# Backward attention of a two-block network: dq and dk accumulated in one pass, and the gradient of q, k, v passed on through DRAM

## The chip, the cores and the metric

The kernel runs on one core of a Trainium2 chip. The metric is device time in microseconds (us) for one launch: the median of several executions. The profile is taken from one further execution, which has a time of its own.

In what follows PE is the matrix engine, DVE the vector engine, ACT the scalar engine, POOL and SP the two others, which here mostly issue transfers. PSUM is the memory that PE writes its results to, in float32; SBUF is the large on-chip memory. DRAM is the chip's main memory.

## The reference

Four residual blocks, A, B, A, B, on x of shape [1, 2048, 576] in bf16, and the gradient of the result with respect to x and all five weights. Block A is attention with 32 heads of 18 elements, in which each position looks at itself and seven earlier ones at a distance of two:

```python
W, dil = 8, 2
q, k, v = qkv[0], qkv[1], qkv[2]
off = jnp.arange(W) * dil
idx = pos[:, None] - off[None, :]
mask = idx >= 0
kg = k[:, :, idx_c, :].reshape(B, H, S, W, Dh)
vg = v[:, :, idx_c, :].reshape(B, H, S, W, Dh)
logits = jnp.einsum("bhsd,bhswd->bhsw", q, kg) * scale
attn = _softmax(jnp.where(mask, logits, -1e9), axis=-1)
o = jnp.einsum("bhsw,bhswd->bhsd", attn, vg)
```

Block B is a bilinear unit with 4608 hidden columns: (x Wg) * (x Wu), times Wd. Both blocks are preceded by a layer norm without weights.

For the backward pass of A let dl[s,w] be the gradient of the logits. Then dq[s] = scale * sum over w of dl[s,w] * k[s-2w], dk[s] = sum over w of dl[s+2w,w] * q[s+2w], with the scale folded into the stored q, and dv[s] = sum over w of attn[s+2w,w] * do[s+2w]. The sum for dq reads k shifted back; those for dk and dv gather from later positions. The gradients of q, k and v together, called dqkv, are multiplied by the transposed weights to give dh, the gradient of the layer norm's output, and are used once more at the end for the weight gradients.

## The kernel before

The kernel runs forward through the layers, and then backward: layer 3 (B), layer 2 (A), layer 1 (B), layer 0 (A). The weight gradients of B and then of A come last. The change lies in the backward pass of A, `layer_A_bwd` (L640), which runs twice, for l=2 and l=0.

Feature rows are laid out transposed: features on partitions, positions along a row. The 576 features form five chunks, four of 126 rows (seven heads) and one of 72 (four heads). The 2048 positions form four groups of 512 columns, written `sg`, and 16 tiles of 128, written `t`. q, k and v in this layout make 15 chunks, numbered `jc`, five each for q, k and v.

The stages of `layer_A_bwd`, in order:

- The transposed weights `WqkvT` and `WoT` are loaded (L655, L658), or built the first time.
- The gradient of the block's output is transposed and multiplied by `WoT`, which gives `doT`. The attention weights are loaded transposed into `attnT`.
- `load_T` (L706) loads the stored v, k or q rows, with zeroed pads left and right, in five transfers that alternate between the queues of ACT and POOL (L712). Its pool has one buffer, so each load has to wait until the last user of the one before is done.
- The dl stage (L717 to L747) multiplies `doT` by shifted v on DVE (L726), sums over each head on PE (L730), and forms the logit gradients with the attention weights `attn_t` (L735). They go to DRAM (L746), and come back transposed as `dlT` (L748).
- Three accumulation passes, `attn_acc_pass` (L226): dv from `attnT` and `doT`, dq from `dlT` and k, dk from `dlT` and q. The k rows are loaded after the dv pass in the text, the q rows after the dq pass.
- 15 writes (L766) copy the finished rows, 504 KB each, to `dqkvT_s` in DRAM for the weight gradients. `dq()` deals them out, two in three to POOL's queue and one in three to ACT's.
- The dh stage (L770 to L782) has for each of the 16 tiles 15 matmuls of 512 and 15 of 64 columns (L775), which read `dqkvT` as their stationary operand, then the evacuation to `dh_sb` (by `evac`, L168 on DVE and L170 on ACT), and the layer norm's backward `ln_bwd_tile`.

An accumulation pass has 80 tasks: for each of the five chunks, each of the four column groups, and each of four pairs of w. Four tasks, one group in the text below, add up into one accumulator. A task is:

- two broadcast matmuls (L251) that spread the values of the 32 heads over the 18 rows of each head, into two PSUM banks, `bc2`
- a cast by ACT to bf16, `bcb` (L279)
- a product on DVE with two shifted windows of the second factor at once (L280). The operand's outer step of -2 or +2 elements makes the two windows overlap
- two matmuls with the identity (L285), which add the products into a PSUM accumulator

For every fourth task (`DVE_DIRECT = 4`) the cast is left out and DVE multiplies directly from PSUM (L276). After the fourth task of a group `dst_fn`, made by `mk_dst` (L749), evacuates the accumulator on DVE into `dqkvT` (L755, and with a scale for dq L757). `dqkvT` is an SBUF tile of 15 x 2048 bf16 values in each partition, 60 KB.

In the "plus" passes the broadcast window is shifted along with the product's window, so that the gathered product already stands at its destination column. In the "minus" pass (dq) the broadcast window isn't shifted.

A pass broadcasts two tasks ahead of the products (`lead=2`). A scheduler fixes the order on each engine when the program is built, and sets the semaphores; each engine then works in that order. Pools give out buffers in turn, and a tile that takes memory of an earlier one waits for its last user.

Of the kernel before, what the change touches and what calls it, by code (L numbers as in the profile page):

```python
# [20 lines left out]
FG = 4  # L21
POOL_EW = False
DVE_DIRECT = 4
BC_FULLK = True


# [66 lines left out]
class Kern:  # L93
# [128 lines left out]
        eng.memset(tl[:, :, PL + d.S:d.PW], 0.0)  # L222

    def attn_acc_pass(self, name, bcT, mulT, mode, dst_fn, post_fn=None, lead=2, group_fn=None):  # L226
        nc, tc, d = self.nc, self.tc, self.d
# [7 lines left out]
        with tc.tile_pool(name=f"{name}_psbc", bufs=lead + 1, space=bass.MemoryType.PSUM) as bcp, \  # L235
# [6 lines left out]
            def emit_bc(k):  # L242
# [18 lines left out]
            def emit_rest(k):  # L261
# [12 lines left out]
                prod = pw.tile([P, 2, d.GW], BF16, tag="prod2")  # L274
                if DVE_DIRECT and k % DVE_DIRECT == DVE_DIRECT - 1:
                    nc.vector.tensor_tensor(out=prod[:nr], in0=bc2[:nr], in1=shifted, op=ALU.mult)  # L276
# [363 lines left out]
    def layer_A_bwd(self, l, a):  # L640
        nc, tc, d = self.nc, self.tc, self.d
        A_wqkv, A_wo = self.aps["A_wqkv"], self.aps["A_wo"]
        out_2, out_3 = self.aps["out_2"], self.aps["out_3"]
        ch = d.chunks
        JCH = [(qkv, c, h0, nh, r0, nr) for qkv in range(3) for (c, h0, nh, r0, nr) in ch]
        with ExitStack() as es:
            keep = es.enter_context(tc.tile_pool(name=f"Ab{l}_keep", bufs=1))
            WqkvT = keep.tile([P, 3 * d.NCH, d.D], BF16, name="WqkvT")
            WoT = keep.tile([P, d.NCH, d.D], BF16, name="WoT")
            dlT = keep.tile([P, 2, d.PW], BF16, name="dlT")  # L650
            self.zero_pads(nc.gpsimd, dlT, 2)
            if self._wA_built:
                for jc, (qkv, c, h0, nh, jr0, jr) in enumerate(JCH):
                    eng = nc.scalar if jc % 2 == 0 else nc.gpsimd
                    eng.dma_start(out=WqkvT[:jr, jc, :], in_=self.WqkvT_d[jc, :jr, :])  # L655
                for (kc, _, _, kr0, kr) in ch:
                    eng = nc.scalar if kc % 2 == 0 else nc.gpsimd
                    eng.dma_start(out=WoT[:kr, kc, :], in_=self.WoT_d[kc, :kr, :])  # L658
            else:
                with tc.tile_pool(name=f"Ab{l}_w", bufs=1) as wpool, \  # L660
# [5 lines left out]
                    for jc, (qkv, c, h0, nh, jr0, jr) in enumerate(JCH):  # L666
                        ps = wps.tile([P, d.D], BF16, tag="wT")
# [5 lines left out]
                    for (kc, _, _, kr0, kr) in ch:  # L673
                        ps = wps.tile([P, d.D], BF16, tag="wT")
# [4 lines left out]
                        nc.gpsimd.dma_start(out=self.WoT_d[kc, :kr, :], in_=WoT[:kr, kc, :])  # L679
                self._wA_built = True  # L680
            with ExitStack() as esA:
                pA = esA.enter_context(tc.tile_pool(name=f"Ab{l}_pA", bufs=1))
                dqkvT = pA.tile([P, 3 * d.NCH, d.S], BF16, name="dqkvT")
                with ExitStack() as es1:
                    p1 = es1.enter_context(tc.tile_pool(name=f"Ab{l}_p1", bufs=1))
                    doT = p1.tile([P, d.NCH, d.PW], BF16, name="doT")
# [3 lines left out]
                    with tc.tile_pool(name=f"Ab{l}_dyT", bufs=1) as dytp:  # L690
                        dyT = dytp.tile([P, d.NCH, d.S], BF16, name="dyT")
                        self.cast_transpose_phase(l, dyT)
                        with tc.tile_pool(name=f"Ab{l}_dops", bufs=2, space=bass.MemoryType.PSUM) as dops:
                            for (c, h0, nh, r0, nr) in ch:
                                for sg in range(d.NG):
                                    s0 = sg * d.GW
                                    ps = dops.tile([P, d.GW], FP32, tag="dops")
                                    for (kc, _, _, kr0, kr) in ch:
                                        nc.tensor.matmul(ps[:nr, :], lhsT=WoT[:kr, kc, r0:r0 + nr],  # L699
                                                         rhs=dyT[:kr, kc, s0:s0 + d.GW],  # L700
                                                         start=(kc == 0), stop=(kc == d.NCH - 1))
# [13 lines left out]
                    with tc.tile_pool(name=f"Ab{l}_lps", bufs=1, space=bass.MemoryType.PSUM) as lpool, \  # L715
                            tc.tile_pool(name=f"Ab{l}_atp", bufs=3) as atp:
                        for sg in range(d.NG):  # L717
                            s0 = sg * d.GW
                            lps = [lpool.tile([P, d.W, d.H], FP32, tag=f"dps{tt}", name=f"dps{tt}") for tt in range(d.G)]
                            k = 0  # L720
                            for w in range(d.W):
                                for (c, h0, nh, r0, nr) in ch:
                                    prod = work.tile([P, d.GW], BF16, tag="prod")
                                    eng = nc.gpsimd if (POOL_EW and k % 3 == 2) else nc.vector
                                    k += 1
                                    eng.tensor_tensor(out=prod[:nr, :], in0=doT[:nr, c, PL + s0:PL + s0 + d.GW],  # L726
                                                      in1=vT[:nr, c, PL + s0 - d.DIL * w:PL + s0 - d.DIL * w + d.GW],
                                                      op=ALU.mult)
                                    for tt in range(d.G):
                                        nc.tensor.matmul(lps[tt][:, w, h0:h0 + nh], lhsT=prod[:nr, tt * P:(tt + 1) * P],  # L730
                                                         rhs=self.IND[:nr, 0:nh], start=True, stop=True)
                            for tt in range(d.G):
                                t = sg * d.G + tt
                                attn_t = atp.tile([P, d.W, d.H], BF16, tag="attn_t")
                                nc.scalar.dma_start(out=attn_t[:].rearrange("p w h -> p (w h)"),  # L735
                                                  in_=self.attn_d[a][t * P:(t + 1) * P, :])
# [12 lines left out]
                    def mk_dst(qkv_out, scale):  # L749
                        def dst_fn(cinfo, sg, accap):  # L750
                            (c, h0, nh, r0, nr) = cinfo
                            j0 = sg * d.GW
                            dst = dqkvT[:nr, qkv_out * d.NCH + c, j0:j0 + d.GW]
                            if scale is None:
                                nc.vector.tensor_copy(out=dst, in_=accap)  # L755
                            else:
                                nc.vector.tensor_scalar_mul(out=dst, in0=accap, scalar1=scale)  # L757
# [9 lines left out]
                with tc.tile_pool(name=f"Ab{l}_dhps", bufs=2, space=bass.MemoryType.PSUM) as dhps, \  # L767
                        tc.tile_pool(name=f"Ab{l}_hn", bufs=2) as hnp, \
                        tc.tile_pool(name=f"Ab{l}_dhsb", bufs=2) as dhsb:
                    for t in range(d.NT):  # L770
                        dh_sb = dhsb.tile([P, d.D], FP32, tag="dh_sb")
                        for (o0, on) in d.dn:
                            ps = dhps.tile([P, 512], FP32, tag="dhps")
                            for jc, (qkv, c, h0, nh, jr0, jr) in enumerate(JCH):
                                nc.tensor.matmul(ps[:, :on], lhsT=dqkvT[:jr, jc, t * P:(t + 1) * P],  # L775
                                                 rhs=WqkvT[:jr, jc, o0:o0 + on],
                                                 start=(jc == 0), stop=(jc == len(JCH) - 1))
                            self.evac(out=dh_sb[:, o0:o0 + on], in_=ps[:, :on], dve_every=3)
                        hn_t = hnp.tile([P, d.D], BF16, tag="hn_t")
                        nc.scalar.dma_start(out=hn_t[:], in_=self.hn_d[l][t * P:(t + 1) * P, :])  # L780
                        self.ln_bwd_tile(hnp, l, t, dh_sb[:], hn_t[:])
        return  # L782

    def dw_phase_B(self, apps):
# [219 lines left out]
```

## Time and profile before

| what | value |
|---|---|
| median of six executions | 4843.29 us (4819.85 to 4861.86) |
| the profiled execution | 4852.41 us |
| its span in the trace | 4850.7 us |
| its mean granted PE clock | 0.921 |
| backward A, l=2: last evacuations of dv, dq, dk | 2427.34, 2506.52, 2587.14 us |
| backward A, l=0: the same | 3441.26, 3520.43, 3600.80 us |
| dh stage, l=2: first matmul, first evacuation | 2586.94, 2590.38 us |
| PE, DVE, ACT busy over the whole span | 87%, 36%, 27% |

The trace gives for each instruction its start, its length, the engine and the line in the code. The length of a DVE or ACT instruction is a little more than the distance at which the next one can follow, since they overlap at their ends; so distances between starts are used where work is back to back. The busy share of the whole span is a mean over stages with different limits. The two attention stages of the backward pass together are about a fifth of the span (about 2180 to 2655 us and 3200 to 3673 us).

### The profile page before, as it was taken

What the parts mean: (1) busy time and instruction counts of PE and PEld (TensorE: products, weight loads), DVE (VectorE), ACT (ScalarE), POOL (GpSimd) and SP (SyncE); (2) the same over time, 40 slices, a digit from 0 to 9 for tenths busy, and PEclk for the clock granted to TensorE, in tenths of its full rate; (3) what the DMA queues carried; (4) which work ended last, traced back from release to release, by engine and by line L of the source; (5) the groups of instructions that cost most, each with busy time, mean ns of one, the idle gap of its engine ahead of it and who ended that gap; (6) DMA issues with size and microseconds to landing.
All of it is one profiled execution on the core that took longest, in us unless ns stands there. A gap on an engine that the chain in (4) does not pass through costs nothing.

```text
span 4850.7 us, 60099 instructions
## 1 busy us (share of the span) xinstructions
PE 4222.1 (87%) x23924; PEld 2338.9 (48%) x23992; DVE 1761.6 (36%) x3795; ACT 1299.8 (27%) x1944; POOL 436.2 (9%) x744
## 2 busy tenths in 40 slices
PE   6689999789998499896798799976985999999978
PEld 4444445444444355444454455544543666655545
DVE  3961113781111133235897133338982000000000
ACT  3243333253333222111474122122751000000000
POOL 3010001000000111011000111110000000000002
PEclk8699999699999799996899899986997999999989
DMA  4046664127666799972112999951117777776692
GB/s 139 10 151 224 216 220 162 40 62 248 205 205 200 229 248 238 216 207 89 53 53 56 234 249 236 232 152 49 35 51 197 141 136 142 136 138 146 136 221 58
DMA packets 1241392, 747.35 MB, mean 154 GB/s; under 512 B 906894, under 2 KB 1187713, under 8 KB 1239958
## 3 DMA queue, kind: packets, MB, share of 16 engines
q1 hardware_dynamic: 969288, 317.17, 30.4%
q10 hardware_dynamic: 211486, 221.88, 15.8%
q0 software_dynamic: 60336, 204.45, 12.7%
q8 instruction: 188, 3.08, 0.3%
q14 instruction: 94, 0.77, 0.1%
HBM read 241.57 MB, written 278.20 MB: 107 GB/s over the span
## 4 chain that ended last, share of the span: by engine, by line
PE 34%; issue 16%; DVE 6%; DMA 5%; ACT 4%; POOL 2%; ACTq 0%; SPq 0%; POOLq 0%; DVEq 0%
PE acc L285 3%; ACT bcb L279 2%; PE ps L609 2%; DMA wuT<-in_B_w_up_dram 1%; PE ps L699 1%; DVE prod L726 1%; ACT dhh L170 1%; DVE dgT L614 1%; DVE prod L280 1%; DVE junk L536 1%; DMA hn_t<-hn_d 1%; DMA tl<-qkvT_d 0%; POOL duT_s L624 0%; DVE xres L543 0%; DMA sl<-oT_d 0%
## 5 line engine op out<-in xcount | busy, mean ns | idle before, releaser
L827 PEld LDWEIGHTS <-hn_sb 128*126 128x126 bf16 (+1 forms) x2880 | 379.5, 132 | 293.6 <-issue 53.0
L285 PE MATMUL acc<-prod,ident 126*126 126x512 bf16 (+1 forms) x1280 | 368.1, 381 | 24.2 <-DVE prod L280 11.4
L170 ACT CAST dhh<-ps 128x512 bf16<-128x512 f32 x288 | 168.6, 586 | 794.4 <-PE ps L609 691.0
L614 DVE TENSOR_TENSOR dgT<-dhh,uq 128x512 bf16<-128x512 bf16 x288 | 121.9, 424 | 705.2 <-ACT dhh L170 686.6
L461 PE MATMUL ps<-hnT,wu 126*128 126x512 bf16 (+1 forms) x1440 | 360.9, 380 | 10.7 <-DMA wu<-in_B_w_up_dram 10.7
L461 PE MATMUL ps<-hnT,wg 126*128 126x512 bf16 (+1 forms) x1440 | 361.4, 381 | 5.9 <-DMA hn_d<-hn_t 3.4
L609 PE MATMUL ps<-dyT,WdT 126*128 126x512 bf16 (+1 forms) x1440 | 343.7, 380 | 1.1 <-ACT dhh L170 1.1
L466 DVE TENSOR_TENSOR hhq<-gsb,usb 128x512 bf16<-128x512 bf16 x288 | 122.5, 425 | 530.3 <-ACT usb L170 528.5
L618 PEld LDWEIGHTS <-wgT 128*126 128x126 bf16 (+1 forms) x1440 | 190.3, 132 | 211.9 <-issue 94.1
L478 PE MATMUL ps<-Wd_sb,hhq 128*128 128x512 bf16 (+1 forms) x2272 | 280.7, 285 | 1.8
L170 ACT CAST gsb<-ps 128x512 bf16<-128x512 f32 x288 | 168.8, 586 | 356.8 <-PE ps L461 348.1
L620 PEld LDWEIGHTS <-wuT 128*126 128x126 bf16 (+1 forms) x1440 | 189.4, 132 | 146.3 <-DMA wuT<-in_B_w_up_dram 23.8
L251 PEld LDWEIGHTS <-INDTq 128*126 128x126 bf16 (+1 forms) x1280 | 168.8, 133 | 186.5 <-issue 67.3
L285 PEld LDWEIGHTS <-ident 126*126 126x126 bf16 (+1 forms) x1280 | 166.6, 131 | 164.4 <-issue 62.8
L461 PEld LDWEIGHTS <-wu 126*128 126x128 bf16 (+1 forms) x1440 | 138.8, 97 | 189.9 <-DMA wu<-in_B_w_up_dram 21.8
L461 PEld LDWEIGHTS <-wg 126*128 126x128 bf16 (+1 forms) x1440 | 140.0, 98 | 178.1 <-issue 9.5
L609 PEld LDWEIGHTS <-WdT 126*128 126x128 bf16 (+1 forms) x1440 | 139.2, 97 | 164.9 <-issue 1.3
L856 PEld LDWEIGHTS <-sl 128*128 128x128 bf16 x2304 | 147.1, 98 | 140.5 <-issue 5.1
L478 PEld LDWEIGHTS <-hhq 128*128 128x128 bf16 x2304 | 147.5, 98 | 138.0 <-issue 0.2
L170 ACT CAST usb<-ps 128x512 bf16<-128x512 f32 x288 | 168.8, 586 | 161.8 <-PE ps L461 161.8
L280 DVE TENSOR_TENSOR prod<-bcb,tl 126x1024 bf16<-126x1024 bf16 (+1 forms) x240 | 163.0, 687 | 22.3 <-ACT bcb L279 19.6
L336 PE MATMUL ps<-hnT,Wqkv_sb 126*126 126x512 bf16 (+1 forms) x600 | 134.7, 387 | 6.2 <-ACT hnT L170 6.2
(2898 smaller groups left out, 7440.4 us busy)
## 6 DMA issues: line engine op xcount, KB each, us to landing
gT_d<-gsb SPq DMA_DIRECT2D x72, 512.0 KB
uT_d<-usb POOLq DMA_DIRECT2D x72, 512.0 KB, 6.8
hhT_d<-hhq SPq DMA_DIRECT2D x72, 512.0 KB
gq<-gT_d ACTq DMA_DIRECT2D x72, 512.0 KB
uq<-uT_d ACTq DMA_DIRECT2D x72, 512.0 KB
dgT_s<-dgT POOLq DMA_DIRECT2D x72, 512.0 KB, 7.0
duT_s<-duT POOLq DMA_DIRECT2D x72, 512.0 KB, 8.0
wg<-in_B_w_gate_dram ACTq DMA_DIRECT2D x72, 504.0 KB
```

What stands on the lines that cost most here:

```text
L170: self.nc.scalar.copy(out=out, in_=in_)
L251: nc.tensor.matmul(bc2[:nr, i, :], lhsT=self.INDTq[:, w % 4, r0:r0 + nr], rhs=bcT[:, w // 4, PL + b0:PL + b0 + d.GW], start=True, stop=True)
L280: nc.vector.tensor_tensor(out=prod[:nr], in0=bcb[:nr], in1=shifted, op=ALU.mult)
L285: nc.tensor.matmul(acc[:nr, :], lhsT=self.ident[:nr, :nr], rhs=prod[:nr, i, :], start=(wp == 0 and i == 0), stop=(wp == NP2 - 1 and i == 1))
L461: nc.tensor.matmul(ps[:, :], lhsT=wt[:kr, kc, i * P:(i + 1) * P], rhs=hnT[:kr, kc, s0:s0 + d.GW], start=(kc == 0), stop=(kc == d.NCH - 1))
L478: nc.tensor.matmul(ps[:, :on], lhsT=hhq[:, fc, tt * P:(tt + 1) * P], rhs=Wd_sb[:, fc, o0:o0 + on], start=(fc == 0), stop=(fc == d.FC - 1))
L609: nc.tensor.matmul(ps[:, :], lhsT=WdT[:kr, kc, fc * P:(fc + 1) * P], rhs=dyT[:kr, kc, s0:s0 + d.GW], start=(kc == 0), stop=(kc == d.NCH - 1))
L614: nc.vector.tensor_tensor(out=dgT[:, i, :], in0=dhh[:], in1=uq[:, i, :], op=ALU.mult)
L618: nc.tensor.matmul(acc[c][:nr, :], lhsT=wgT[:, i, r0:r0 + nr], rhs=dgT[:, i, :], start=(fc == 0), stop=False)
L620: nc.tensor.matmul(acc[c][:nr, :], lhsT=wuT[:, i, r0:r0 + nr], rhs=duT[:, i, :], start=False, stop=(fc == d.FC - 1))
L827: nc.tensor.matmul(acc[c][:nr, :jn], lhsT=hn_sb[:, i, t, r0:r0 + nr], rhs=sls[i][:, t, :jn], start=(k == 0), stop=(k == nstep - 1))
L856: nc.tensor.matmul(acc2[:, :on], lhsT=sls[i][:, t, ii * P:(ii + 1) * P], rhs=dy_bf[:, i, t, o0:o0 + on], start=(k == 0), stop=(k == nstep ...
```

## The change

The passes for dq and dk become one, `attn_dqdk_pass`. It makes the unshifted broadcast of a task once, casts it once, and multiplies it on DVE twice: by two shifted windows of k, as before, and by the unshifted window of q, read twice by an operand with an outer step of zero. The products with k are added up as before. Those with q have to be shifted when they are added: the matmul with the identity reads the product from column `sh` = 2w on and adds to columns 0 to 512 - sh of the group's accumulator. The first `sh` columns belong to the end of the column group before and are added by a small matmul to that group's accumulator, which therefore stays open for one group longer. The pass has no direct products from PSUM, one accumulator buffer for dq and two for dk, and `lead=1`.

`dqkvT` as an SBUF tile goes. Each evacuation, in all passes, writes into a staging tile `st` of 512 columns from a pool of four, and a transfer of 126 KB takes it to `dqkvT_s` at once. The dh stage reads them back: for each column group, 15 transfers, alternating between ACT and POOL, fill `dqb`, one of two buffers, and four tiles are computed from it. The pool of `load_T` gets two buffers. The line numbers of the changed program are larger by some 75 to 90 in this part.

```diff
+    def attn_dqdk_pass(self, name, dlT, kT, qsT, dq_dst, dk_dst, lead=1):
+        tasks = [(ci, sg, wp) for ci in range(len(ch)) for sg in range(d.NG) for wp in range(NP2)]
+        with tc.tile_pool(name=f"{name}_psbc", bufs=lead + 1, space=bass.MemoryType.PSUM) as bcp, \
+                tc.tile_pool(name=f"{name}_psq", bufs=1, space=bass.MemoryType.PSUM) as accq_p, \
+                tc.tile_pool(name=f"{name}_psk", bufs=2, space=bass.MemoryType.PSUM) as acck_p, \
+                tc.tile_pool(name=f"{name}_bcs", bufs=3) as bcs, \
+                tc.tile_pool(name=f"{name}_pw", bufs=3) as pw:
...
+                for i in range(2):
+                    w = 2 * wp + i
+                    nc.tensor.matmul(bc2[:nr, i, :], lhsT=self.INDTq[:, w % 4, r0:r0 + nr],
+                                     rhs=dlT[:, w // 4, PL + j0:PL + j0 + d.GW], start=True, stop=True)
...
+                nc.scalar.copy(out=bcb[:nr], in_=bc2[:nr])
+                w0 = 2 * wp
+                basek = kT[:nr, c, PL + j0 - d.DIL * w0:PL + j0 - d.DIL * w0 + d.GW]
...
+                shk = bass.AP(tensor=basek.tensor, offset=basek.offset, ap=[apl[0], [-d.DIL, 2], apl[1]])
...
+                nc.vector.tensor_tensor(out=prodq[:nr], in0=bcb[:nr], in1=shk, op=ALU.mult)
+                baseq = qsT[:nr, c, PL + j0:PL + j0 + d.GW]
...
+                shq = bass.AP(tensor=baseq.tensor, offset=baseq.offset, ap=[apl2[0], [0, 2], apl2[1]])
...
+                nc.vector.tensor_tensor(out=prodk[:nr], in0=bcb[:nr], in1=shq, op=ALU.mult)
...
+                for i in range(2):
+                    w = w0 + i
+                    sh = d.DIL * w
+                    last_pair = (wp == NP2 - 1 and i == 1)
+                    nc.tensor.matmul(aq[:nr, :], lhsT=self.ident[:nr, :nr], rhs=prodq[:nr, i, :],
+                                     start=(wp == 0 and i == 0), stop=last_pair)
+                    stop_main = last_pair and (sg == d.NG - 1)
+                    nc.tensor.matmul(ak[:nr, 0:d.GW - sh], lhsT=self.ident[:nr, :nr], rhs=prodk[:nr, i, sh:d.GW],
+                                     start=(wp == 0 and i == 0), stop=stop_main)
+                    if sg > 0 and sh > 0:
+                        nc.tensor.matmul(akp[:nr, d.GW - sh:d.GW], lhsT=self.ident[:nr, :nr], rhs=prodk[:nr, i, 0:sh],
+                                         start=False, stop=last_pair)
+                if wp == NP2 - 1:
+                    dq_dst(ch[ci], sg, aq[:nr, :])
+                    del accq[(ci, sg)]
+                    if sg > 0:
+                        dk_dst(ch[ci], sg - 1, akp[:nr, :])
+                        del acck[(ci, sg - 1)]
+                    if sg == d.NG - 1:
+                        dk_dst(ch[ci], sg, ak[:nr, :])
...
-                pA = esA.enter_context(tc.tile_pool(name=f"Ab{l}_pA", bufs=1))
-                dqkvT = pA.tile([P, 3 * d.NCH, d.S], BF16, name="dqkvT")
+                stq = esA.enter_context(tc.tile_pool(name=f"Ab{l}_stq", bufs=4))
...
-                    qkp = es1.enter_context(tc.tile_pool(name=f"Ab{l}_qkv", bufs=1))
+                    qkp = es1.enter_context(tc.tile_pool(name=f"Ab{l}_qkv", bufs=2 if MERGED_DQDK else 1))
...
-                            dst = dqkvT[:nr, qkv_out * d.NCH + c, j0:j0 + d.GW]
+                            jc = qkv_out * d.NCH + c
+                            st = stq.tile([P, d.GW], BF16, tag="st")
                             if scale is None:
-                                nc.vector.tensor_copy(out=dst, in_=accap)
+                                nc.vector.tensor_copy(out=st[:nr, :], in_=accap)
                             else:
-                                nc.vector.tensor_scalar_mul(out=dst, in0=accap, scalar1=scale)
+                                nc.vector.tensor_scalar_mul(out=st[:nr, :], in0=accap, scalar1=scale)
+                            self.dq().dma_start(out=self.dqkvT_s[a][jc * P:jc * P + nr, j0:j0 + d.GW], in_=st[:nr, :])
...
                     kT = load_T(1)
-                    self.attn_acc_pass(f"Ab{l}_dqp", dlT, kT, "minus", mk_dst(0, d.scale))
                     qsT = load_T(0)
-                    self.attn_acc_pass(f"Ab{l}_dkp", dlT, qsT, "plus", mk_dst(1, None))
-                for jc in range(3 * d.NCH):
-                    jr = JCH[jc][5]
-                    self.dq().dma_start(out=self.dqkvT_s[a][jc * P:jc * P + jr, :], in_=dqkvT[:jr, jc, :])
+                    if MERGED_DQDK:
+                        self.attn_dqdk_pass(f"Ab{l}_dqk", dlT, kT, qsT, mk_dst(0, d.scale), mk_dst(1, None))
...
+                    for sg in range(d.NG):
+                        j0 = sg * d.GW
+                        dqb = dqbp.tile([P, 3 * d.NCH, d.GW], BF16, tag="dqb")
+                        for jc, (qkv, c, h0, nh, jr0, jr) in enumerate(JCH):
+                            eng = nc.scalar if jc % 2 == 0 else nc.gpsimd
+                            eng.dma_start(out=dqb[:jr, jc, :], in_=self.dqkvT_s[a][jc * P:jc * P + jr, j0:j0 + d.GW])
+                        for tt in range(d.G):
...
-                                nc.tensor.matmul(ps[:, :on], lhsT=dqkvT[:jr, jc, t * P:(t + 1) * P],
+                                    nc.tensor.matmul(ps[:, :on], lhsT=dqb[:jr, jc, tt * P:(tt + 1) * P],
```

More of the change, by code (lines that the diff above doesn't have):

```diff
@@ L23 @@
 DVE_DIRECT = 4
+MERGED_DQDK = True
 BC_FULLK = True
@@ L222, in zero_pads, with emit_bc, emit_rest @@
         eng.memset(tl[:, :, PL + d.S:d.PW], 0.0)
+    def attn_dqdk_pass(self, name, dlT, kT, qsT, dq_dst, dk_dst, lead=1):
+        nc, tc, d = self.nc, self.tc, self.d
+        ch = d.chunks
+        NP2 = d.W // 2
+        tasks = [(ci, sg, wp) for ci in range(len(ch)) for sg in range(d.NG) for wp in range(NP2)]
[4 more added lines that the diff above has]
+                tc.tile_pool(name=f"{name}_pw", bufs=3) as pw:
+            bc_tiles = {}
+            accq = {}
+            acck = {}
+            def emit_bc(k):
+                ci, sg, wp = tasks[k]
+                (c, h0, nh, r0, nr) = ch[ci]
+                j0 = sg * d.GW
+                bc2 = bcp.tile([P, 2, d.GW], FP32, tag="bc2")
+                for i in range(2):
+                    w = 2 * wp + i
+                    nc.tensor.matmul(bc2[:nr, i, :], lhsT=self.INDTq[:, w % 4, r0:r0 + nr],
+                                     rhs=dlT[:, w // 4, PL + j0:PL + j0 + d.GW], start=True, stop=True)
+                bc_tiles[k] = bc2
+            def emit_rest(k):
+                ci, sg, wp = tasks[k]
+                (c, h0, nh, r0, nr) = ch[ci]
+                j0 = sg * d.GW
+                bc2 = bc_tiles.pop(k)
+                bcb = bcs.tile([P, 2, d.GW], BF16, tag="bcb")
+                nc.scalar.copy(out=bcb[:nr], in_=bc2[:nr])
+                w0 = 2 * wp
+                basek = kT[:nr, c, PL + j0 - d.DIL * w0:PL + j0 - d.DIL * w0 + d.GW]
+                apl = [list(x) for x in basek.ap]
+                shk = bass.AP(tensor=basek.tensor, offset=basek.offset, ap=[apl[0], [-d.DIL, 2], apl[1]])
+                prodq = pw.tile([P, 2, d.GW], BF16, tag="prodq")
+                nc.vector.tensor_tensor(out=prodq[:nr], in0=bcb[:nr], in1=shk, op=ALU.mult)
+                baseq = qsT[:nr, c, PL + j0:PL + j0 + d.GW]
+                apl2 = [list(x) for x in baseq.ap]
+                shq = bass.AP(tensor=baseq.tensor, offset=baseq.offset, ap=[apl2[0], [0, 2], apl2[1]])
+                prodk = pw.tile([P, 2, d.GW], BF16, tag="prodk")
+                nc.vector.tensor_tensor(out=prodk[:nr], in0=bcb[:nr], in1=shq, op=ALU.mult)
+                if wp == 0:
+                    accq[(ci, sg)] = accq_p.tile([P, d.GW], FP32, tag="accq", name="accq")
+                    acck[(ci, sg)] = acck_p.tile([P, d.GW], FP32, tag="acck", name="acck")
+                aq = accq[(ci, sg)]
+                ak = acck[(ci, sg)]
+                akp = acck.get((ci, sg - 1)) if sg > 0 else None
+                for i in range(2):
[18 more added lines that the diff above has]
+                        dk_dst(ch[ci], sg, ak[:nr, :])
+                        del acck[(ci, sg)]
+            for k in range(len(tasks) + lead):
+                if k < len(tasks):
+                    emit_bc(k)
+                j = k - lead
+                if j >= 0:
+                    emit_rest(j)
@@ L735, in layer_A_bwd @@
                                 nc.scalar.dma_start(out=attn_t[:].rearrange("p w h -> p (w h)"),
-                                                  in_=self.attn_d[a][t * P:(t + 1) * P, :])
+                                                    in_=self.attn_d[a][t * P:(t + 1) * P, :])
                                 tmp = atp.tile([P, d.W, d.H], FP32, tag="sb_tmp")
@@ L760, in layer_A_bwd @@
                     kT = load_T(1)
-                    self.attn_acc_pass(f"Ab{l}_dqp", dlT, kT, "minus", mk_dst(0, d.scale))
                     qsT = load_T(0)
-                    self.attn_acc_pass(f"Ab{l}_dkp", dlT, qsT, "plus", mk_dst(1, None))
-                for jc in range(3 * d.NCH):
-                    jr = JCH[jc][5]
-                    self.dq().dma_start(out=self.dqkvT_s[a][jc * P:jc * P + jr, :], in_=dqkvT[:jr, jc, :])
+                    if MERGED_DQDK:
+                        self.attn_dqdk_pass(f"Ab{l}_dqk", dlT, kT, qsT, mk_dst(0, d.scale), mk_dst(1, None))
+                    else:
+                        self.attn_acc_pass(f"Ab{l}_dqp", dlT, kT, "minus", mk_dst(0, d.scale))
+                        self.attn_acc_pass(f"Ab{l}_dkp", dlT, qsT, "plus", mk_dst(1, None))
@@ L767, in layer_A_bwd @@
                 with tc.tile_pool(name=f"Ab{l}_dhps", bufs=2, space=bass.MemoryType.PSUM) as dhps, \
+                        tc.tile_pool(name=f"Ab{l}_dqb", bufs=2) as dqbp, \
                         tc.tile_pool(name=f"Ab{l}_hn", bufs=2) as hnp, \
                         tc.tile_pool(name=f"Ab{l}_dhsb", bufs=2) as dhsb:
[L770 to L781, printed above, removed]
@@ new lines, in layer_A_bwd @@
+                    for sg in range(d.NG):
+                        j0 = sg * d.GW
+                        dqb = dqbp.tile([P, 3 * d.NCH, d.GW], BF16, tag="dqb")
[3 more added lines that the diff above has]
+                        for tt in range(d.G):
+                            t = sg * d.G + tt
+                            dh_sb = dhsb.tile([P, d.D], FP32, tag="dh_sb")
+                            for (o0, on) in d.dn:
+                                ps = dhps.tile([P, 512], FP32, tag="dhps")
+                                for jc, (qkv, c, h0, nh, jr0, jr) in enumerate(JCH):
+                                    nc.tensor.matmul(ps[:, :on], lhsT=dqb[:jr, jc, tt * P:(tt + 1) * P],
+                                                     rhs=WqkvT[:jr, jc, o0:o0 + on],
+                                                     start=(jc == 0), stop=(jc == len(JCH) - 1))
+                                self.evac(out=dh_sb[:, o0:o0 + on], in_=ps[:, :on], dve_every=3)
+                            hn_t = hnp.tile([P, d.D], BF16, tag="hn_t")
+                            nc.scalar.dma_start(out=hn_t[:], in_=self.hn_d[l][t * P:(t + 1) * P, :])
+                            self.ln_bwd_tile(hnp, l, t, dh_sb[:], hn_t[:])
```

## The prediction

> **What bounds the kernel now.** The change lies inside the backward pass of the two attention layers (l=2 and l=0), so I read that stage. First the page's busy shares: over the whole span PE is busy 87%, DVE 36%, which says nothing about this stage. Then busy time by window, for the dv, dq and dk passes of l=2, the dh stage and the gap behind it; columns are window, length, then busy us (count) of PE, PEld, DVE, ACT, POOL, then granted clock, DMA share, GB/s:
>
> ```profile
> 2346.00:2427.00 81.00, 74.52 (x317) 41.80 (x316) 72.44 (x99) 57.10 (x60) 1.08 (x2) 0.96 0.15 40
> 2427.00:2507.00 80.00, 74.20 (x326) 42.18 (x325) 73.44 (x101) 56.92 (x60) 2.92 (x8) 1.00 0.12 34
> 2507.00:2587.00 80.00, 72.57 (x319) 41.29 (x318) 72.19 (x100) 57.01 (x60) 2.03 (x4) 1.00 0.20 60
> 2587.00:2655.00 68.00, 61.66 (x481) 31.43 (x479) 51.86 (x116) 20.22 (x37) 1.05 (x2) 1.00 0.14 40
> ```
>
> Two engines are nearly full in each pass, PE 92% and DVE 91%. The timeline of DVE over one group of four tasks in the dq pass shows the beat (start, length, engine, line, tile):
>
> ```profile
> 2437.65 0.69 DVE L757 TENSOR_SCALAR dqkvT<-acc 126x512 bf16<-126x512 f32 x1
> 2438.25 0.68 DVE L280 TENSOR_TENSOR prod<-bcb,tl 126x1024 bf16<-126x1024 bf16 x1
> 2438.85 1.22 DVE L276 TENSOR_TENSOR prod<-bc_20832,tl 126x1024 bf16<-126x1024 f32 x1
> 2439.99 0.69 DVE L280 TENSOR_TENSOR prod<-bcb,tl 126x1024 bf16<-126x1024 bf16 x1
> 2440.90 0.69 DVE L280 TENSOR_TENSOR prod<-bcb,tl 126x1024 bf16<-126x1024 bf16 x1 [0.22 <-ACT bcb L279]
> 2441.51 0.68 DVE L757 TENSOR_SCALAR dqkvT<-acc 126x512 bf16<-126x512 f32 x1
> ```
>
> From starts: a bf16 product or an evacuation follows its predecessor after 0.60 us, the product read from PSUM (L276) takes 1.14. A group is 3x0.60 + 1.14 + 0.60 = 3.54 us of DVE, and its real pitch is 2441.51 - 2437.65 = 3.86. PE has 16 matmuls of 512 columns in a group, 0.2165 each back to back, 3.46. So PE and DVE alternate in holding the beat, with 0.3 to 0.4 lost in handing over.
>
> **The pass.** From the last evacuation of dv (2427.34) to the last of dk (2587.14; call that moment E) dq and dk take 159.80 us at l=2, 159.54 at l=0. The merged pass makes 20 groups instead of 40:
> - DVE: 8 products and 2 evacuations a group. No product reads PSUM any more, so all cost 0.60: 10x0.60 = 6.0 us.
> - PE: 8 broadcast matmuls (they were 16 for the two groups), 8 for dq, 8 for dk, so 24x0.2165 = 5.2, and for 15 of 20 groups 7 tails of 2 to 14 columns. The nearest row is L730's 7-column matmuls, 0.028 to 0.03 apart: 0.2. Sum 5.4.
> - ACT: 4 casts at a pitch of 0.91, 3.64, and two thirds of a DMA issue at 0.33: 3.9.
>
> DVE becomes the bound, with 0.6 us over PE. Work alone: 20x6.0 + 1.6 (dv's last evacuation to the first dq product now) = 121.6. For handover: at present a group takes 3.86/3.54 = 1.09 times its DVE work, but that is with PE at the same load. The compiled order of the changed program puts each group's products as q0, k0, q1, k1 and so on, with evacuations a product or two later, and broadcasts three to four tasks ahead; with the durations above I found no wait on DVE. I take a third of the old overhead, 3%: 123.6 + 1.6 = 125.2. **Saving 34.5 us a layer**; ends 121.6 (38.1) and 1.09x120 + 1.6 = 132.4 (27.3).
>
> The prodk product is an unknown: its second operand has an outer step of zero (one q row read twice). The nearest rows are L280's with outer steps of +2 or -2 elements, read overlapping, at 0.69 us. [...]
>
> Between dq and dk a second stall goes. At the boundary at l=0 DVE waited for the q rows, whose single buffer came free only when dq ended:
>
> ```profile
> 3523.73 1.90 DVE L280 TENSOR_TENSOR prod<-bcb,tl 126x1024 bf16<-126x1024 bf16 x3 [2.62 <-DMA tl<-qkvT_d]
> ```
>
> It is inside the 159.7 already. With two buffers both loads are issued far ahead. The price is at the dl stage's start, where k rows now load beside v rows, for which DVE waits 9 us (2248 to 2257): the k issues stand behind v's in their queues, so sharing costs 0 to 2; I take 0.5.
>
> **Streaming out.** 60 evacuations a layer each issue a write of 126 KB instead of 15 of 504 KB at the end. POOL (0.52 an issue, under 3 us busy in 80) has room. A staging tile comes round after four evacuations, two groups or 12 us; the nearest landings are 1.9 us (64 KB) and 2.5 (144 KB), so no evacuation waits. Without that cover it would be some 2.5 a group. ACT's third stands 1.5 groups behind its evacuation and holds no cast. Nothing.
>
> **Streaming in: dh start.** Now the first dh matmul needs no transfer:
>
> ```profile
> 2586.94 3.86 PE L775 MATMUL ps<-WqkvT,dqkvT 126*128 126x512 bf16 x30
> 2587.14 0.69 DVE L755 CAST dqkvT<-acc 72x512 bf16<-72x512 f32 x1 [0.68 <-PE acc L285]
> ...
> 2590.38 0.70 ACT L170 COPY dh_sb<-ps 128x512 f32<-128x512 f32 x2 [6.08 <-PE ps L775]
> ```
>
> First evacuation at E + 3.24. Afterwards it needs 15 loads of 126x1 KB. Five (jc 0 to 4) are issued 3 to 6 us before E; the rest stand behind the last evacuations' writes. On POOL, write, 5, 7, the last write (at E), then 9, 11, 13, so the last issue is about E + 0.1 + 4x0.52 = E + 2.1; ACT is done sooner. The nearest row for such loads is the reload of WqkvT at l=0, 15 loads of up to 141.8 KB on the same two queues:
>
> ```profile
> L655 ACTq DMA_DIRECT2D WqkvT<-WqkvT_d x8: 333/390/414, 3221.1 to 3224.1; - x8
> L655 POOL DMA_DIRECT2D WqkvT<-WqkvT_d x7: 530/532/673, 3221.4 to 3224.6; - x7
> DMA to landing us min/median/max: 3.5/5.0/6.8
> ```
>
> So the last lands at E + 6 to 7.5 and, with most matmuls still to run, the evacuation comes near E + 7.7: **+4.5 a layer**, 2 to 10.
>
> [...] The trace's row is 2.0 MB within about 10 us (3221.1 to 3224.6 plus 6.8), some 200 GB/s, since many are under way together. I take the row.
>
> Clock: PE will idle some 4 to 6 us there. The trace shows what idling does, at the dl start (idle from 2247.9) and behind the attn_t wait (busy from 2345.2); the last figures of a line are clock, DMA share, GB/s:
>
> ```profile
> 2251.00:2252.00 1.00, 0.00 (x0) 0.00 (x0) 0.14 (x1) 0.00 (x0) 0.00 (x0) 1.00 0.91 373
> 2253.00:2254.00 1.00, 0.00 (x0) 0.00 (x0) 0.00 (x0) 0.00 (x0) 0.00 (x0) 0.50 0.96 246
> 2350.00:2351.00 1.00, 1.00 (x3) 0.46 (x2) 1.00 (x2) 0.14 (x1) 0.00 (x0) 0.50 1.27 290
> 2352.00:2353.00 1.00, 1.00 (x6) 0.56 (x5) 0.60 (x1) 0.70 (x1) 0.00 (x0) 1.00 0.19 40
> ```
>
> The clock halves 5 us after PE stops and returns 6.6 us after it resumes, a loss of 3.3. [...] Half: **+1.5**, 0 to 3.3.
>
> **Streaming in: the rest of dh.** A 512-column set lasts 4 tiles x 4.24 = 17 us. Set 1's buffer lies over the q rows, free at E. Sets 2 and 3 wait for PE to leave their buffer; POOL queues nothing behind them but its next loads. 7x0.52 + 5 to 7 of landing, with room for contention, is 9 to 13.5 of 17: hidden. Eight issues of 0.33 a set stand on ACT between dh_sb evacuations, which PE (two PSUM buffers) and ln_bwd wait for: **+1.0** a layer, 0 to 3. The WdT reload waits for the last dh matmul as now (its memory lies under the new buffers too): 0 +- 3.
>
> **Sum.** -34.5 + 4.5 + 1.5 + 1.0 + 0.5 = -27.0 a layer, -54 for two. The profiled execution took 4852.4 (span 4850.7 and 1.7 around it), so 4798; it stood 9 above the median, 4843.3, so **4789**.
>
> **Rivals.**
> - *Handovers take the slack.* The merged pass is written to look ahead one task, not two, has one dq accumulator, and PE still queues ident matmuls that wait for DVE ahead of broadcasts; for it, today's 0.3 to 0.4 a group. Against: DVE's new lead over PE. At 6.9 a group: 139.6, a saving of 20.1, net -12.6 a layer, 4818.
> - *Each set's load is exposed.* If sets 1 to 3 arrive 7 us late (landing 10 and more, the issues stuck on ACT), +21: -6 a layer, 4831. [...]
> - *Slower:* the zero step loses prodk its fast rate. A group is 6x0.60 + 4x1.14 = 8.16, the pass 164.8, +5.1 and 7.5 for the dh costs: +12.6 a layer, **4868**. It turns slower once the pass takes over 152.2, a group over 7.53.
> - *The gain doesn't appear:* the broadcast, cast and direct-read savings are real in the program's order, so this lives only in the rivals above.
>
> **Chances.** Forecast 0.65 (own range 4770 to 4808), handovers 0.17, exposed loads 0.10, slow prodk 0.08. The bound is 0.5%, 24 us, about what six runs spread over 0.9% can tell. Faster: 0.63 of the forecast, 0.09 and 0.02 of the next two, 0.74 to 0.75. Slower: 0.08, and 0.02 of mishaps in the others. The range runs from the forecast's best end (pass 121.6, dh +2, 4770, less 10 for the spread) to the exposed case and a little over.
>
> **What will show it.** prodk's and prodq's rows at 0.69; evacuation pitch of dq 6.0 to 6.5; dv's last to the last dk evacuation 122 to 132; first dh_sb evacuation 5 to 11 after it, with a wait for dqb on PE; later dh tiles 4.2 to 4.4 apart without DMA waits. A prodk of 1.2 us, a pitch over 6.9, or PE waiting for dqb at each set would make this wrong.

## The result, and the profile after

| | before | changed |
|---|---|---|
| median | 4848.58 us (20 runs, 4819.85 to 4864.57) | 4808.27 us (10 runs, 4787.20 to 4854.53) |
| profiled execution, span | 4852.41, 4850.7 | 4869.98, 4868.3 |

The ratio is 0.9933, with a 95% interval of 0.9905 to 0.9962: faster by 0.67%, some 32 us, between 18 and 46. The ratio weighs all runs; the two medians alone lie 40 apart. The forecast was 54. The profiled execution of the changed kernel took 62 us more than its median, and 20 of these lie ahead of the first changed instruction (the first matmul on WoT of l=2 starts at 2243.9 us, before at 2223.2). So in what follows stages are compared, not spans. The trace of a later kernel that differs only in the queue of the loads ("The loads on SP" below), from an execution of 4791 us, has the same stages within 2 us.

The stages of the backward attention layers, from the two traces, l=2 / l=0, in us. E is, as in the prediction, the moment of the last dk evacuation; an accumulation matmul of the B layer is called dhacc after its tile:

| stage | before | changed | sum of both layers |
|---|---|---|---|
| last dhacc matmul of the B layer to the first on WoT | 50.8 / 31.7 | 50.6 / 53.6 | +21.6 |
| dl: first product to last dl_t | 92.3 / 91.5 | 96.3 / 94.2 | +6.7 |
| last dv evacuation to last dk evacuation (E) | 159.8 / 159.5 | 122.9 / 123.5 | -72.9 |
| E to the first dh_sb evacuation | 3.2 / 3.3 | 10.9 / 10.4 | +14.8 |
| from there to the last dh matmul | 63.6 / 66.5 | 68.2 / 66.2 | +4.3 |
| last dh matmul to the first on WdT (l=2) | 29.8 | 24.9 | -4.9 |

With -0.6 from the rest (doT and dv) this adds up to -31, which is what the runs show. The merged pass brings a little more than forecast, and over half of it is given back in four places. The largest of them, the first row, is not in the prediction.

**The pass.** The timeline of DVE over one group of the merged pass, and windows from there to the dh stage (columns as in the prediction):

```profile
2464.36 0.68 DVE L265 TENSOR_TENSOR prodq<-bcb,tl 126x1024 bf16<-126x1024 bf16 x1
2464.95 0.68 DVE L835 CAST st<-acck 126x512 bf16<-126x512 f32 x1
2465.55 0.68 DVE L270 TENSOR_TENSOR prodk<-bcb,tl 126x1024 bf16<-126x1024 bf16 x1
2466.15 0.68 DVE L265 TENSOR_TENSOR prodq<-bcb,tl 126x1024 bf16<-126x1024 bf16 x1
2466.75 0.69 DVE L270 TENSOR_TENSOR prodk<-bcb,tl 126x1024 bf16<-126x1024 bf16 x1
...
2470.37 0.69 DVE L837 TENSOR_SCALAR st<-accq 126x512 bf16<-126x512 f32 x1
```

```profile
2471.00:2491.00 20.00, 19.08 (x95) 11.56 (x94) 20.00 (x35) 13.92 (x15) 3.18 (x6) 1.00 0.16 44
2491.00:2511.00 20.00, 19.18 (x99) 11.87 (x98) 20.00 (x34) 13.65 (x14) 2.12 (x4) 1.00 0.17 48
...
2566.00:2571.00 5.00, 4.37 (x23) 2.03 (x22) 5.00 (x10) 2.02 (x3) 0.53 (x1) 1.00 0.11 30
2571.00:2576.00 5.00, 3.09 (x12) 1.24 (x12) 3.07 (x5) 0.00 (x0) 3.25 (x7) 0.54 0.45 141
2576.00:2591.00 15.00, 13.15 (x42) 4.81 (x43) 2.44 (x6) 1.48 (x3) 5.17 (x10) 0.50 0.91 234
...
2594.00:2600.00 6.00, 5.78 (x40) 2.85 (x39) 4.51 (x13) 1.96 (x3) 0.00 (x0) 1.00 0.10 25
```

prodk, with its outer step of zero, takes the 0.69 us of prodq. DVE is busy 20.00 of 20.00, and no line of the group shows a wait: from the first to the last dq evacuation 19 groups take 2572.60 - 2458.63 = 113.97 us, 6.00 each, exactly ten operations of 0.60.

**The start of dh.** The last four windows show PE's clock falling to half and coming back. The trace's clock records put the fall at 2571.4, 2.7 us before E (2574.1), and the return at 2591.9; at l=0 it fell 3.9 us before E and stayed at half as long, 20.5 us. ACT over that time, a product on DVE, the last, and the landing of POOL's loads between 2570 and 2585:

```profile
2572.18 1.20 ACTq L857 DMA_DIRECT2D dqb<-dqkvT_s  x3
2574.22 0.32 ACTq L838 DMA_DIRECT2D dqkvT_s<-st  x1
2574.64 2.21 ACTq L857 DMA_DIRECT2D dqb<-dqkvT_s  x5
...
2585.06 0.58 ACT L171 COPY dh_sb<-ps 128x512 f32<-128x512 f32 x1 [15.45 <-DMA dqb<-dqkvT_s]
```

```profile
2571.43 0.67 DVE L270 TENSOR_TENSOR prodk<-bcb,tl 72x1024 bf16<-72x1024 bf16 x1
```

```profile
DMA to landing us min/median/max: 3.1/6.6/7.7
```

The first load goes out at 2572.18. The last product ends at 2571.43 + 0.67 = 2572.10. So even the first five loads, whose data had been written before, waited for the last product. By POOL's landings the first set's last piece on that queue (jc 13) was issued at E + 2.8 and landed at E + 9.8, 1.2 us before the first evacuation. POOL issued the second set right behind, from 2577.46 on, and the 234 GB/s of the window 2576 to 2591 are those of both sets together.

**The start of the attention layer at l=0.** This is where nothing was expected. Before, SP issued the transposing load of attnT (start, length of the issue) as soon as the B layer's last dhacc matmul, which began at 3206.45 and takes 0.38, was done. In the changed kernel it goes out only with the loads of WqkvT, which ACT issues at 3242.96:

```profile
3206.86 5.71 SPq L703 DMA_TRANSPOSE attnT<-attn_d  x1
```

```profile
3243.00 15.05 SPq L782 DMA_TRANSPOSE attnT<-attn_d  x1
```

What that does to WqkvT is seen in the transfers of both kernels (issuing queue, number, size, median us from issue to landing), first before, then changed:

```profile
WqkvT<-WqkvT_d POOLq DMA_DIRECT2D x6, 141.8 KB, 4.7
```

```profile
WqkvT<-WqkvT_d POOLq DMA_DIRECT2D x6, 141.8 KB, 25.7
WoT<-WoT_d POOLq DMA_DIRECT2D x2, 141.8 KB, 22.8
```

And ACT's timeline in the changed kernel:

```profile
3246.30 0.90 ACTq L735 DMA_DIRECT2D WqkvT<-WqkvT_d  x2
3273.52 1.18 ACTq L738 DMA_DIRECT2D WoT<-WoT_d  x3
3274.74 1.01 ACT L171 COPY dyT<-cpst_26880 126x1024 bf16<-126x1024 bf16 x1 [27.72 <-DMA WoT<-WoT_d]
```

The transfers land some 20 us later, and so does the transpose: by the packets of its queue it runs from 3244.60 to 3272.91, 28.3 us, instead of 6.0 (3208.48 to 3214.50). What ACT waits for is the transpose. Its first issue for WoT waits on the semaphore that tells of the transpose's landing (the program deals out the same few semaphores in turn, and the trace has number 102 at both), and goes out 0.6 us after the transpose's last packet. The three other kernels that stream, below, show the same: one semaphore at both, and 0.6 us. Behind that issue stand dyT's evacuations, for which PE waits. ACT is idle for 27.7 us and the layer starts 21.9 us later than before. At l=2 the transpose goes out late too (2229.6 instead of 2172.7), but there the weights are built on the chip and ACT issues no such load; that stage kept its length.

The table of waits says what the transpose itself waited for in the changed kernel:

```profile
SPq L782 <- DVE dhT_sb L169: 32.0, 1, 32.0
SPq L782 <- PE dh_ps L714: 12.4, 1, 12.4
```

These are the last operations of the B layer. The built programs tell why. Without dqkvT's 60 KB below them the tiles of the attention layer moved down in SBUF. Before, attnT took bytes 178432 to 186752 of each partition, where the B layer's wuT buffers had been; their last reader is the last dhacc matmul, and the transpose waited for that. In the changed kernel it takes 121088 to 129408, inside the place of the B layer's WdT (85312 to 131392). WdT shares a pool with dhT_sb, and the transpose's semaphores wait for that pool's last reader, the last dh_ps transpose. No run changed the place of attnT alone.

### The profile page after: what moved, and what is told of

Same layout as the page of the kernel before. It is cut to its first block, busy times and chain, and to the rows that moved or that the text cites. A ratio compares the mean times of both kernels' runs of the same rounds, so it can differ in the third digit from the quotient of the medians.

```text
span 4868.3 us, 59964 instructions
## 1 busy us (share of the span) xinstructions
PE 4186.9 (86%) x23814; PEld 2321.1 (48%) x23882; DVE 1711.0 (35%) x3795; ACT 1231.7 (25%) x1864; POOL 498.2 (10%) x860
## 5 line engine op out<-in xcount | busy, mean ns | idle before, releaser
L365 PE MATMUL acc<-prod,ident 126*126 126x512 bf16 (+1 forms) x640 | 187.1, 385 | 10.3 <-DVE prod L356 5.4
L864 PE MATMUL ps<-WqkvT,dqb 126*128 126x512 bf16 (+3 forms) x960 | 138.5, 302 | 18.9 <-ACT dh_sb L171 6.7
L702 POOL DMA_DIRECT2D dgT_s<-dgT x72 | 54.2, 753 | 977.9 <-DVE dgT L694 915.0
L331 PEld LDWEIGHTS <-INDTq 128*126 128x126 bf16 (+1 forms) x640 | 85.9, 136 | 110.6 <-issue 42.9
```

What stands on the lines that cost most here:

```text
L365: nc.tensor.matmul(acc[:nr, :], lhsT=self.ident[:nr, :nr], rhs=prod[:nr, i, :], start=(wp == 0 and i == 0), stop=(wp == NP2 - 1 and i == 1))
L864: nc.tensor.matmul(ps[:, :on], lhsT=dqb[:jr, jc, tt * P:(tt + 1) * P], rhs=WqkvT[:jr, jc, o0:o0 + on], start=(jc == 0), stop=(jc == len(JC ...
```

## The experiments

All times against the kernel before on the same chip, with the 95% interval of the ratio.

**Merging alone.** dqkvT stays in SBUF, and nothing is streamed. The rows keep their single buffer beside dqkvT, and q goes into the tile of doT once the dv pass is done with it. `attn_dqdk_pass` is that of the change.

```diff
                     kT = load_T(1)
-                    self.attn_acc_pass(f"Ab{l}_dqp", dlT, kT, "minus", mk_dst(0, d.scale))
-                    qsT = load_T(0)
-                    self.attn_acc_pass(f"Ab{l}_dkp", dlT, qsT, "plus", mk_dst(1, None))
+                    for (c, h0, nh, r0, nr) in ch:
+                        eng = nc.scalar if c % 2 == 0 else nc.gpsimd
+                        eng.dma_start(out=doT[:nr, c, PL:PL + d.S], in_=self.qkvT_d[a][0, c, :nr, :])
+                    self.attn_dqdk_pass(f"Ab{l}_dqk", dlT, kT, doT, mk_dst(0, d.scale), mk_dst(1, None))
```

> Before, with the two passes merged and nothing streamed: dqkvT stays in SBUF, and the q rows are loaded into doT's tile once dv is done, so they may be exposed at the start of the merged pass. If streaming is what gives part of the gain back: dv's last to dk's last evacuation 122 to 128 us (the changed kernel's is 123, plus up to 4 for the q load), first dh_sb evacuation 3.3 after it as before, dl stage (first product to last dl_t) 92 as before; some 33 to 36 a layer, in all -65 to -72, near 4780. If the gain is small for another reason (memory that is reused later, the B stages): the same pass, but in all -30 to -45, as the changed kernel.

Measured: 4760.90 (5 runs), before 4836.68, ratio 0.9837 [0.9800, 0.9874]. That is 79 us, more than twice the gain of the full change and a little over the 65 to 72 expected, and the best kernel of this study. Stages, l=2 / l=0: dl 93.0 / 92.9, pass 122.7 / 122.7, E to the first dh_sb 1.9 / 1.9, last dhacc matmul to the first on WoT 50.4 / 32.8. The pass is the changed kernel's, and of the give-backs what is left is about 1 us in each dl stage and in the last of these, and 3.5 in the rest of dh at l=2. The gap to WdT is 20.7 instead of 29.8, which wasn't traced; those 9 us make up most of what was not expected. The q load isn't exposed. PE's timeline at its end, and the windows there:

```profile
2531.34 0.17 PE L285 MATMUL acck<-prodk,ident 72*72 72x14 bf16 x1
2531.37 2.79 PE L854 MATMUL ps<-WqkvT,dqkvT 126*128 126x512 bf16 x13
```

```profile
2532.00:2534.00 2.00, 2.00 (x11) 0.90 (x10) 0.96 (x2) 0.00 (x0) 0.53 (x1) 1.00 0.63 177
2534.00:2536.00 2.00, 1.75 (x22) 1.05 (x21) 1.07 (x2) 0.70 (x2) 0.00 (x0) 1.00 0.86 257
```

Three dh matmuls ran before these lines already, from 2528.39 on, between the last accumulations. The others follow the last accumulation after 0.03 us, 0.9 before E (2532.3), and the clock stays at 1.00. That even beats the 3.2 and 3.3 of before, since of three evacuations behind the last products two start after the last accumulation, while PE is free.

**Streaming alone.** The changed kernel with the two passes of before.

```diff
-MERGED_DQDK = True
+MERGED_DQDK = False
```

> The changed kernel with dq and dk in two passes as before, one buffer for the v, k and q rows, and the streaming through DRAM. If streaming costs what the profile of the changed kernel shows: passes 159.5 together, first dh_sb evacuation about E + 10 instead of E + 3.3, dh stage 7 to 12 longer a layer, dl stage as before; in all +14 to +24 us over before. If streaming is free and the merged pass's end (an idle PE, the halved clock) makes the late dh start: within 4 us of before a layer.

Measured: 4886.69 (12 runs), ratio 1.0094 [1.0060, 1.0128]: 46 us slower than before, about twice what was expected. The expected part is there: dl 92.8 / 93.0 (one buffer, so no k load beside v), E to the first dh_sb 12.3 / 11.6, dh from E on 11 and 5 us longer. dq and dk take 163.5 / 161.5, 2 to 4 more than before. The unexpected part is the start of the attention layer at l=0, 50.2 us instead of 31.7. SP's issue of the transposing load, and WqkvT's transfers beside it:

```profile
3264.69 14.44 SPq L782 DMA_TRANSPOSE attnT<-attn_d  x1
```

```profile
WqkvT<-WqkvT_d POOLq DMA_DIRECT2D x6, 141.8 KB, 22.7
```

So the late transpose belongs to the streaming, not to the merged pass, and it is no accident of one execution: it is in all four kernels that stream (53.6, 50.2, 51.7 and 50.4 us) and in neither that doesn't (31.7 and 32.8). And with the passes as before, dh starts as late (E + 12.3 and 11.6) and the clock halves too (at l=2 0.50 from 2602 to 2616); the merged pass's end is not the cause.

**The loads on SP.** The changed kernel, and all of dqb on a queue that holds nothing else then.

```diff
-                            eng = nc.scalar if jc % 2 == 0 else nc.gpsimd
+                            eng = nc.sync
```

> The changed kernel with all dqb loads on SP's queue, which holds nothing else there: no load stands behind an evacuation's write on POOL or ACT. If the order of issue makes dh start late: first dh_sb evacuation at E + 4 to 6.5 instead of E + 10 to 11, the clock back earlier, 4 to 8 us less a layer than the changed kernel. If the landing of the last pieces or the halved clock alone sets it: E + 9 to 11 and no change. SP issues all 15 one after another, so above 0.5 an issue it could be later too.

Measured: 4807.28 (12 runs), ratio 0.9933 [0.9905, 0.9961], as the changed kernel. First dh_sb evacuation at E + 10.6 / 10.4: the order on POOL and ACT isn't what makes it late.

```profile
2532.17 15.30 SPq L857 DMA_DIRECT2D dqb<-dqkvT_s  x30
```

```profile
2531.36 0.68 DVE L270 TENSOR_TENSOR prodk<-bcb,tl 72x1024 bf16<-72x1024 bf16 x1
```

The first line is SP's queue, the second DVE's last product. On an idle queue, too, the first load waits for the last product (2531.36 + 0.68 = 2532.04), 1.9 us before E. The first buffer lies where doT was, which nothing reads after the dv pass. But the pool of the two buffers, bytes 100288 to 131008, reaches with its last 1600 bytes into the tile of the q rows (from 129408), which the last product reads, and the wait is taken for the pool as a whole: in a program built with one buffer the same load waits only for a product of the dv pass. From there it is the landing of the loads: ACT's first evacuation waits 15.1 us, by the trace for dqb. The clock alone doesn't decide the first evacuation: at l=0 of this kernel it was back at full 7.2 us after E, and the evacuation still came at E + 10.4. That an earlier buffer would bring dh forward was not tried; nor was keeping PE busy through the gap, or loading k after the dl stage in the streaming kernel.

**dk's evacuations on ACT.** If DVE alone bounds the merged pass, one operation less of ten should show.

```diff
-                                nc.vector.tensor_copy(out=st[:nr, :], in_=accap)
+                                (nc.scalar.copy if qkv_out == 1 else nc.vector.tensor_copy)(out=st[:nr, :], in_=accap)
```

> The changed kernel with dk's evacuations on ACT instead of DVE. If DVE alone bounds the merged pass (20.00 us busy in windows of 20): a group falls from 6.05 to 5.45 until PE's 5.4 takes over, the pass to 109 to 114 us from 123, and 8 to 13 less a layer. If PE and the handovers already set the beat: 119 to 124. ACT has 3.9 of 6 us in a group, 4.6 with the evacuation, so ACT should not become late; if it does, the pass is longer than 123.

Measured: 4812.26 (12 runs), ratio 0.9943 [0.9912, 0.9974]; the pass 121.2 / 121.2 instead of 122.9 / 123.5. The expectation of 109 to 114 failed. The windows, one product that waits, and ACT before it:

```profile
2480.00:2500.00 20.00, 19.82 (x103) 11.92 (x102) 18.94 (x32) 14.56 (x17) 2.12 (x4) 1.00 0.12 34
2500.00:2520.00 20.00, 19.73 (x104) 12.34 (x103) 19.11 (x32) 15.09 (x18) 2.12 (x4) 1.00 0.19 53
```

```profile
2523.41 0.69 DVE L265 TENSOR_TENSOR prodq<-bcb,tl 126x1024 bf16<-126x1024 bf16 x1 [0.84 <-ACT bcb L259]
```

```profile
2521.39 1.07 ACT L835 CAST st<-acck 126x512 bf16<-126x512 f32 x2 [0.67 <-PE acck L287]
...
2522.35 1.03 ACT L259 CAST bcb<-bc 126x1024 bf16<-126x1024 f32 x1
```

Nine operations are 5.4 us, and PE's work is 5.4 too, by the sum in the prediction (24 matmuls at 0.2165 and 0.2 for the tails). The 19 groups between the first and last dq evacuation take 5.92 each (2456.37 to 2568.80), 1.10 times the work of either. Where the rest goes can be added up from the timeline. DVE stands idle for 9.8 us in these 19 groups. In 6.9 of them it waits for a cast that directly follows a dk evacuation on ACT, and in 2.7 a dq evacuation waits for PE. In the lines above ACT waits 0.67 us for the end of an accumulation, evacuates twice, and only then makes the cast that DVE needs. So the move took 0.6 us a group from DVE and gave back 0.36 of it through the order of work on ACT, though ACT was busy for 14.6 of 20 only. Whether PE and DVE at equal work would have lost time without that, as the 1.09 of before (3.86 over 3.54) suggests, this run doesn't tell.

**Adding up.** The stage sums (from each B layer's last dhacc matmul to the last dh matmul, and the gap to WdT) against the runs, in us, to before:

| kernel | stages | runs, ratio x 4848 |
|---|---|---|
| changed | -31 | -32 |
| merging alone | -82 | -79 |
| streaming alone | +37 | +46 |
| loads on SP | -33 | -32 |
| dk's evacuation on ACT | -39 | -28 |

The intervals of the runs are some 15 us to either side, so within them the stages account for all five.

## Why the prediction was right or wrong

The sign and the range held; the size didn't: 54 was forecast, 32 came, and 4808 is the slow end of the range that was given to the forecast itself (4770 to 4808). The time alone would have fitted the handover rival (4818) better. The stages tell what happened:

- **The pass:** 34.5 a layer forecast, 36.9 and 36.0 measured. DVE as the bound at 6.0 was right. The allowance of 3% for handovers was too much; there was none. With the broadcasts and casts halved DVE didn't wait for them any more. What made the 1.09 of before isn't shown: the run with ACT's evacuations lost a like share (1.10), but most of it to the order of work on ACT.
- **The zero step of prodk:** 0.69 us long and 0.60 to the next start, as the nearest row (L280) had it; that rival is out. The handover rival is out as well for this kernel, at 6.00 a group.
- **Streaming out at nothing:** no evacuation in the merged pass waits for its staging tile; right there. Streaming alone took 2 to 4 us more over dq and dk, which wasn't traced further.
- **The start of dh:** +4.5 and +1.5 forecast, +7.7 and +7.1 measured. The step that failed is "five (jc 0 to 4) are issued 3 to 6 us before E". They went out 1.9 before E, since their pool reached into the q rows' tile; the prediction saw that overlap and took it for the second set alone. The queues behind them slid with them: the last issue on POOL came at E + 2.8, not E + 2.1. The larger miss is the landing, 7.0 us for that piece, where E + 6 to 7.5 allowed 4 to 5.4: the row of 200 GB/s held as a rate (234 in the window 2576 to 2591), but the second set, which wasn't in that sum, shared it. The clock fell 2.7 and 3.9 us before E and stayed at half for 20.5 us at both layers; that half of 3.3 us would be lost to it was an estimate, which no run shows. How much of the stage is the clock's wasn't separated; the first evacuation is not its doing alone (see the loads on SP).
- **The rest of dh:** +1.0 a layer forecast, +4.6 and -0.3 measured. The exposed-loads rival (7 us a set) is out. Both layers ran 6 to 7 us at half clock behind the first evacuation (at l=2 to 2591.9), so that doesn't tell the two apart; before, l=0 took 2.9 longer than l=2. Why is open.
- **The k load beside v:** 0.5 forecast, +4.0 and +2.7 measured. The kernels with one buffer have dl stages of 91.5 to 93.0, the three others with two 94.2 to 96.3. DVE's wait for the v rows grew from 9.0 and 10.3 us to 14.0 and 13.2. "The k issues stand behind v's in their queues" was true and beside the point: POOL's v loads landed 7.1 to 9.9 us after their issue before, and 9.0 to 13.4 with k's under way beside them.
- **Not in the sum at all:** the start of the attention layer at l=0, +21.9, the largest give-back. The prediction followed the instructions that moved, and found none ahead of `layer_A_bwd`'s own stages. But removing dqkvT also moved every later tile in SBUF, and so changed what the transposing load of attnT had to wait for. The prediction weighed this for WdT behind the dh stage (0 +- 3, measured -4.9), and not for the layer's own loads at its start.

Without the last term the sum of the measured ones is -53, next to the forecast of -54. That is luck and not precision: the errors in the pass and at the WdT gap made good those in dh and dl.

## What to carry to other kernels

When a change takes a large tile away, look not only at the instructions that move but at where the remaining tiles now lie: a load that started early, over memory that was read for the last time early, may come to lie where an earlier layer reads to its end, and then goes out together with other loads. When data is streamed out and back, look at what the whole pool of the buffers lies over, not only the first buffer. Here keeping the data on the chip, and finding room for one operand in a tile that had just died, was worth 47 us more than streaming. And an engine with time to spare can still set the pace by the order of its work: with dk's evacuations ahead of the casts on ACT, the pass gained 1.7 to 2.3 us instead of the 9 to 14 expected.

## What the runs showed of the hardware

- Beside a transposing load in flight (1.05 MB), POOL's 141.8 KB transfers took a median of 25.7 us to land instead of 4.7 (22.2 to 25.7 in four kernels), and the transpose 28.3 instead of 6.0. In the two kernels where the transpose went out 14 to 15 us ahead of them they took 4.7 and 4.9.
- PE's clock fell to 0.50 without a full stop. In the window of 5 us before (2566 to 2571) PE was busy 4.37 by the records, in short bursts. It was still at half through 2576 to 2591, with a busy sum of 13.15 of 15. The longest stretch without a matmul in the records is 0.6 us from 2566 to the fall at 2571.4, and 1.4 us from there to 2591. That the short bursts made the clock fall is not shown.
